# One attention + FFN kernel: attention output in natural token order, one store per FFN tile, and a last tile copied by two engines

## The chip, the cores and the metric

The kernel runs on one core of one Trainium2 chip. A core has five engines with instruction streams of their own: PE (TensorE, matmuls), DVE (VectorE), ACT (ScalarE), POOL (GpSimd) and SP (SyncE, which here only issues DMAs). They meet through semaphores. The metric is the device time of one execution in microseconds (us).

## The reference

Decayed linear attention over blocks of 64 tokens (4 batches, 8 heads, 768 tokens, head dimension 64), and on its output an FFN of 3072 tokens with a snake activation:

```python
for b in range(nb):                       # 12 blocks of 64 tokens
    qb, kb, vb = q[:, :, sl], k[:, :, sl], v[:, :, sl]
    intra = einsum('bhic,bhjc->bhij', qb, kb) * Dmask      # lam**(i-j) for i >= j
    intra = einsum('bhij,bhjd->bhid', intra, vb)
    inter = einsum('bhid,bhde->bhie', qb * lam_pow, kv_state)
    out[:, :, sl] = intra + inter
    kv_state = lam_block * kv_state + einsum('bhsd,bhse->bhde', kb * rev_pow, vb)

x = out.transpose(0, 2, 1, 3).reshape(3072, 512)
h = x @ w_in                              # 512 -> 2048
g = h + sin(alpha * h)**2 / (alpha + 1e-09)
y = g @ w_out                             # 2048 -> 512, fp32
```

## The kernel before

**Units and groups.** The attention is done in 24 units. A unit is 256 tokens of one batch and four heads, in two blocks of 128 tokens (index c). Four units (two batches, two halves of the heads) make a group g of 512 tokens; there are six groups. For each group the FFN has 16 FFN1 tiles (f, 128 of the 2048 channels by 512 tokens) and four FFN2 tiles (m, 128 tokens by 512 outputs).

**Tokens in pairs.** A load puts tokens 2p and 2p+1 of a block on the same partition ("(p two) e -> p h (two e)"), which makes 512-byte runs. So inside a block of 128 tokens the columns stand as two runs of 64, first the even tokens ("par" 0), then the odd ones. Before the change this order goes through the whole kernel: the scores, the attention output in PSUM (`okv`), the activations `xt`, the FFN. It is undone when the result is stored: `f2st` (L753) sends a tile in two DMAs, one per parity, of 64 partitions each.

**A unit's steps**, with the names in the written orders: `ldNq/k/v` loads (SP); `cqN`, `ckN` casts to bf16 and `svN` scaling of v (L490 to L498); transposes on PE with copies (`tqN`, `tkN`, `e0N`, `e1N`, L508 to L517) for the first nine units, a DMA transpose `dtN` for the others; `scN` scores (L532); `mmN` mask product (DVE, L540); k-v products (L566) with their copy `kcN` (`kv_copy`, L576, `kva`), `bxN`/`d0N`/`d1N`/`n0N`/`n1N` for the state (`kvbd`, L594, L608); `inN`, `ioN` the two output products (`intermm` L642 and `outmm` L655, both into `okv`); `oeN` the scaled read-out of `okv` by the table `ET` into `xt` (`outev`, DVE, L674). From unit 8 on, the PE part of a unit and the output part of the unit before are one `stepN`.

**FFN steps.** `f1_g_f` (L689, four matmuls), `sn` sine (ACT, L696), `sq` square (ACT L703 or POOL L705), `g_g_f` the product and sum into `gall` (DVE, L708); `f2_g_m_j` (L725, a quarter of the 16 matmuls of a tile), `ev_g_m` the copy of the tile out of PSUM to one of three output buffers `ob` (`f2ev`, L731, ACT), `out_g_m` its store (SP). The last tile (g 5, m 3) is done in two column halves `a` and `b`, with `end0`/`end1` as copies (`f2end`, L737, L739) and `send0`/`send1` as stores (`f2send`, L746). `warm` are filler matmuls (L762) of the start.

**The order.** Each engine's instructions stand in an order written out by hand (`SEQ`), a list of names for each engine. A small planner (`Plan.run`) walks these lists with a cost for each operation and a model of the DMA queues and of instruction fetches (`FETCH`); it only decides which buffer each operation takes and in which global sequence the operations are emitted. On an engine the written order is the order of execution, and so is SP's: a store that waits holds back every load and store behind it. SP's list ends so:

```
out_3_3 out_2_0 out_2_3 out_4_3 out_5_2 out_5_1 send1 send0 out_5_0
```

PE's ends with `f2_5_0_3 f2_5_3_2b f2_5_3_3b`, ACT's with `ev_5_2 end0 ev_5_1 ev_5_0`, DVE's with `g_5_9_None end1`.

Of the kernel before, what the change touches and what calls it, by code (L numbers as in the profile page):

```python
# [10 lines left out]
ALU = mybir.AluOpType  # L11
# [18 lines left out]
class Plan:  # L30
# [5 lines left out]
    FETCH = (4.0, 14.5, 21.5, 27, 48, 56, 66.5, 76.5, 86, 98.5, 108.5, 121, 131.5, 142.5, 157)  # L36
    HOLD, SHARE = 1.5, 0.35
# [108 lines left out]
def kernel(  # L146
# [28 lines left out]
            "warm warm warm warm lamb warm warm warm warm warm warm warm warm warm warm warm tq0 "  # L175
            "warm alpha tk0 warm warm warm tq1 warm tab0 kv0 sc0 tk1 warm tq2 warm warm warm sc1 "
            "warm tk2 kv1 in0 io0 sc2 warm kv2 warm in1 tq3 io1 warm tk3 in2 io2 sc3 kv3 warm warm "
            "tq4 in3 warm warm warm io3 f1_0_0_0 tk4 f1_0_0_1 f1_0_1_None sc4 kv4 f1_0_5_None in4 "
            "f1_0_2_None f1_0_3_None f1_0_4_None io4 f1_0_8_None f1_0_6_None f1_0_7_None f1_0_9_None "
            "f1_0_15_None f1_0_14_None f1_0_13_None f2_0_0_0 f2_0_1_0 f1_0_10_None f1_0_11_None "  # L180
            "f2_0_0_1 f2_0_3_0 f1_0_12_None f2_0_1_1 f2_0_1_2 f2_0_0_2 f2_0_0_3 tq5 f2_0_3_1 tk5 tq6 "
            "f2_0_1_3 sc5 tk6 f2_0_3_2 kv5 sc6 kv6 f2_0_3_3 tq7 in5 io5 tk7 f2_0_2_0 kv7 sc7 "
            "f2_0_2_1 in6 io6 f2_0_2_2 in7 io7 f2_0_2_3 f1_1_8_None f1_1_15_None tq8 f1_1_9_None "
            "f1_1_4_None f1_1_7_None f1_1_1_None f1_1_0_None tk8 f1_1_3_None step8 f1_1_2_None "
            "f1_1_5_None f1_1_10_None f1_1_6_None step9 f1_1_11_None f2_1_2_0 f2_1_0_0 f2_1_2_1 "
            "step10 f1_1_12_None f1_1_13_None f2_1_0_1 f2_1_0_2 step11 f1_1_14_None f2_1_1_0 "
            "f2_1_1_1 f2_1_1_2 step12 f2_1_0_3 f2_1_1_3 f1_2_15_None f1_2_3_None f1_2_4_None step13 "
            "f1_2_5_None f2_1_2_2 f1_2_6_None f2_1_2_3 f1_2_8_None f1_2_14_None f1_2_7_None f2_1_3_0 "
            "f2_1_3_1 step14 f1_2_0_None f1_2_13_None f2_1_3_2 f2_1_3_3 f1_2_12_None f1_2_2_None "
            "step15 f1_2_1_None f1_2_9_None f1_2_10_None step16 f1_2_11_None f2_2_1_0 f2_2_1_1 "  # L190
            "f1_3_15_None step17 f1_3_13_None f2_2_1_2 f1_3_12_None f2_2_1_3 f1_3_3_None f1_3_7_None "
            "f1_3_0_None f1_3_14_None step18 f1_3_11_None f2_2_2_0 f1_3_5_None f2_2_2_1 step19 "
            "f1_3_8_None f1_3_1_None f2_2_2_2 f1_3_10_None f2_2_2_3 step20 f1_3_6_None f1_3_4_None "
            "f1_3_2_None f1_3_9_None step21 f1_4_15_None f1_4_4_None f2_3_1_0 f2_3_1_1 step22 "
            "f1_4_6_None f1_4_11_None f2_3_1_2 f2_3_1_3 step23 f1_4_0_None f1_4_14_None f1_4_1_None "
            "f2_3_0_0 io23 f2_3_0_1 f2_3_0_2 f1_5_15_None f2_3_0_3 f1_5_14_None f1_5_3_None "
            "f1_4_10_None f2_3_2_0 f2_3_2_1 f1_4_5_None f1_4_7_None f2_3_2_2 f2_3_2_3 f1_4_3_None "
            "f1_5_4_None f1_4_12_None f1_4_2_None f2_3_3_0 f2_3_3_1 f1_4_8_None f1_5_6_None f2_3_3_2 "
            "f1_4_9_None f2_3_3_3 f1_4_13_None f2_4_2_0 f2_4_2_1 f1_5_1_None f1_5_8_None f2_4_2_2 "
            "f2_4_2_3 f1_5_12_None f2_4_0_0 f2_4_0_1 f1_5_0_None f2_4_0_2 f2_4_0_3 f2_4_3_0 "  # L200
            "f1_5_5_None f1_5_11_None f2_4_3_1 f1_5_2_None f2_4_3_2 f2_4_1_0 f2_4_1_1 f2_2_0_0 "
            "f2_4_3_3 f2_2_0_1 f1_5_7_None f2_4_1_2 f2_4_1_3 f1_5_13_None f2_2_3_0 f2_2_3_1 "
            "f1_5_10_None f2_2_3_2 f2_2_3_3 f2_2_0_2 f2_2_0_3 f1_5_9_None f2_5_1_0 f2_5_2_0 "
            "f2_5_3_0a f2_5_3_1a f2_5_2_1 f2_5_3_2a f2_5_3_3a f2_5_1_1 f2_5_2_2 f2_5_2_3 f2_5_1_2 "
            "f2_5_0_0 f2_5_1_3 f2_5_3_0b f2_5_3_1b f2_5_0_1 f2_5_0_2 f2_5_0_3 f2_5_3_2b f2_5_3_3b ",
        "DVE":
            "tabc tabm tab2 ck0 alphav tab4 mm0 e02 mm1 oe0 mm2 oe1 e13 oe2 bx3 mm3 oe3 e14 g_0_0_0 "
            "g_0_0_1 bx4 mm4 g_0_1_None g_0_5_None g_0_2_None g_0_3_None g_0_4_None g_0_8_None "
            "g_0_6_None g_0_7_None oe4 g_0_15_None g_0_14_None g_0_9_None g_0_10_None g_0_11_None "
            "g_0_13_None g_0_12_None e15 e06 mm5 bx5 bx6 mm6 oe5 bx7 mm7 oe6 oe7 e08 g_1_8_None "  # L210
            "g_1_15_None g_1_9_None g_1_4_None g_1_7_None e18 g_1_0_None g_1_1_None g_1_3_None mm8 "
            "g_1_5_None g_1_2_None g_1_6_None mm9 oe8 g_1_10_None g_1_11_None oe9 mm10 g_1_13_None "
            "g_1_12_None mm11 oe10 g_1_14_None oe11 mm12 g_2_15_None g_2_3_None g_2_4_None "
            "g_2_5_None mm13 g_2_6_None oe12 g_2_14_None g_2_7_None mm14 oe13 g_2_8_None g_2_0_None "
            "g_2_13_None g_2_12_None mm15 oe14 g_2_2_None g_2_1_None oe15 g_2_10_None mm16 "
            "g_2_11_None g_2_9_None g_3_15_None g_3_13_None mm17 g_3_12_None oe16 g_3_3_None "
            "g_3_7_None g_3_0_None oe17 mm18 g_3_14_None g_3_11_None g_3_5_None oe18 mm19 g_3_8_None "
            "g_3_1_None g_3_10_None oe19 mm20 g_3_4_None g_3_6_None g_3_2_None mm21 oe20 g_3_9_None "
            "g_4_15_None oe21 g_4_4_None mm22 g_4_6_None mm23 g_4_11_None oe22 g_4_1_None oe23 "
            "g_4_14_None g_4_0_None g_5_15_None g_5_14_None g_4_10_None g_5_3_None g_4_7_None "  # L220
            "g_4_5_None g_4_3_None g_5_4_None g_4_2_None g_4_12_None g_4_8_None g_5_6_None "
            "g_4_9_None g_4_13_None g_5_1_None g_5_8_None g_5_0_None g_5_12_None g_5_11_None "
            "g_5_2_None g_5_5_None g_5_7_None g_5_10_None g_5_13_None g_5_9_None end1 ",
        "ACT":
            "lam alq cq0 e00 cq1 e01 e10 kc0 tab3 e11 ck2 e12 kc1 cq3 kc2 ck3 e03 cq4 e04 kc3 "
            "sn_0_0_0 sq_0_0_0 sn_0_0_1 sq_0_0_1 sn_0_1_None kc4 sn_0_5_None sn_0_2_None sn_0_3_None "
            "sn_0_4_None sq_0_3_None sn_0_8_None sn_0_6_None sq_0_6_None sn_0_7_None sq_0_7_None "
            "sn_0_15_None sn_0_14_None sq_0_15_None sn_0_13_None sn_0_9_None sq_0_9_None "
            "sn_0_10_None sq_0_10_None sn_0_11_None sq_0_11_None sn_0_12_None sq_0_12_None cq5 cq6 "
            "e05 ev_0_0 ev_0_1 e16 kc6 kc5 e07 e17 ev_0_3 kc7 cq8 ev_0_2 sn_1_8_None sq_1_8_None "  # L230
            "sn_1_15_None sn_1_9_None sn_1_4_None sq_1_9_None sn_1_7_None sq_1_7_None sn_1_1_None "
            "sn_1_0_None sq_1_0_None sn_1_3_None sq_1_3_None kc8 sn_1_2_None sn_1_5_None sq_1_5_None "
            "sn_1_6_None sq_1_6_None sn_1_10_None kc9 sq_1_10_None sn_1_11_None sq_1_11_None ck12 "
            "kc10 sn_1_12_None sn_1_13_None sq_1_13_None sq_1_12_None kc11 cq13 sn_1_14_None ck13 "
            "sq_1_14_None kc12 cq15 cq14 ev_1_0 ev_1_1 sn_2_15_None sq_2_15_None sn_2_3_None "
            "sn_2_4_None kc13 sn_2_5_None sq_2_4_None sq_2_5_None sn_2_6_None sq_2_6_None ev_1_2 "
            "sn_2_8_None sn_2_14_None sn_2_7_None sq_2_14_None sq_2_7_None kc14 cq18 sn_2_0_None "
            "sn_2_13_None sq_2_0_None sq_2_13_None ev_1_3 sn_2_12_None sq_2_12_None sn_2_2_None kc15 "
            "sq_2_2_None sn_2_1_None sq_2_1_None sn_2_10_None kc16 sn_2_9_None sn_2_11_None "
            "sq_2_11_None ck18 sq_2_9_None sn_3_15_None kc17 sq_3_15_None sn_3_13_None sq_3_13_None "  # L240
            "sn_3_12_None cq20 ev_2_1 sn_3_3_None sn_3_7_None sn_3_0_None sq_3_7_None kc18 "
            "sn_3_14_None sn_3_11_None sq_3_11_None sn_3_5_None cq23 sq_3_5_None kc19 sn_3_8_None "
            "sq_3_8_None sn_3_1_None sn_3_10_None sq_3_1_None sq_3_10_None kc20 ev_2_2 sn_3_6_None "
            "sn_3_4_None sq_3_4_None sn_3_2_None sq_3_2_None sn_3_9_None sq_3_9_None kc21 "
            "sn_4_15_None sn_4_4_None sq_4_15_None kc22 sn_4_11_None sn_4_6_None sq_4_6_None kc23 "
            "ev_3_1 sq_4_11_None sn_4_0_None sn_4_1_None sq_4_1_None sn_4_14_None sq_4_14_None "
            "sn_5_15_None ev_3_0 sq_5_15_None sn_5_14_None sn_4_10_None sq_4_10_None sn_5_3_None "
# [192 lines left out]
    def tables_e(op):  # L440
        A.copy(out=ET[:], in_=tb0.tile[:])

# [629 lines left out]
```

## Time and profile before

| what | value |
|---|---|
| median of 3 runs | 218.9 us (218.4 to 218.98) |
| the profiled execution: its time, its span | 218.37 us, 216.6 us |
| granted TensorE clock, mean | 0.991 |
| busy: PE, DVE, ACT, POOL | 206.4, 119.4, 139.1, 131.4 us |
| filler matmuls (L762) in PE's busy time | 33 matmuls, 8.3 us |
| the chain that ended last, by engine | PE 87%, POOL 5%, DVE 2%, issue 2%, ACT 1% |
| stores | 46 of 128 KB, 4 of 64 KB |
| DMA | 33.65 MB, mean 155 GB/s |

The span goes from the first to the last instruction of the profiled execution; its own time is taken around that. Busy times come from instruction records. Matmul records overlap, as the next one starts before the last column of the one before has come out, so a group's start-to-start distance is its price on PE, not the duration of its records. A wait is put down to what ended it.

### The profile page before, as it was taken

How to read it: one execution, taken by the hardware profiler on the slowest of the kernel's cores; microseconds unless marked ns; L12 is line 12 of the kernel's file. 1: busy time of each engine (PE TensorE's matmuls, PEld its weight loads, DVE VectorE, ACT ScalarE, POOL GpSimd, SP SyncE). 2: the span in 40 equal slices, each digit the busy share in tenths (PEclk: the TensorE clock that was granted, in tenths of full speed). 3: DMA queues.
4: the chain of work that ended last, by engine and by line, in shares of the span. 5: the costliest groups of instructions: out<-in, count | busy, mean ns of one | idle time of the engine just before them, and what ended most of it. 6: DMA issues, size and time to landing. Idle time of an engine off the chain costs nothing.

```text
span 216.6 us, 5232 instructions
## 1 busy us (share of the span) xinstructions
PE 206.4 (95%) x2066; PEld 105.6 (49%) x2066; DVE 119.4 (55%) x174; ACT 139.1 (64%) x251; POOL 131.4 (61%) x212
## 2 busy tenths in 40 slices
PE   8889999999999999999999999999999999999970
PEld 3466444555445555455545555544444444445430
DVE  3487775385488754777958868773555223022000
ACT  3675788554998668979887787567587635442210
POOL 7999899488799789998979998231511120011000
PEclk9999999999999999999999999999999999999996
DMA  6999999999998999999888740042040120044424
GB/s 176 300 278 207 206 157 200 304 251 305 246 278 221 182 273 250 249 190 293 224 201 203 128 100 3 0 100 48 0 97 2 25 61 14 0 97 92 99 55 98
DMA packets 62139, 33.65 MB, mean 155 GB/s; under 512 B 17938, under 2 KB 59170, under 8 KB 62114
## 3 DMA queue, kind: packets, MB, share of 16 engines
q1 hardware_dynamic: 57776, 29.04, 57.9%
q0 software_dynamic: 4224, 4.19, 12.3%
q8 instruction: 16, 0.26, 0.5%
q10 hardware_dynamic: 114, 0.07, 0.1%
q14 instruction: 9, 0.07, 0.1%
HBM read 27.27 MB, written 6.29 MB: 155 GB/s over the span
## 4 chain that ended last, share of the span: by engine, by line
PE 87%; POOL 5%; DVE 2%; issue 2%; ACT 1%; POOLq 0%; DVEq 0%
PE hps L689 38%; PE ops L725 35%; PE okv L725 3%; PE sp L532 3%; PE okv L655 3%; PE okv L642 2%; POOL vb L498 1%; DVE gall L708 1%; PE okv L566 1%; PE pt L508 1%; POOL E L410 1%; ACT s L696 1%; ACT s L703 1%; DVE sm L540 1%; POOL w_in_sb L456 0%
## 5 line engine op out<-in xcount | busy, mean ns | idle before, releaser
L708 DVE SCALAR_TENSOR_TENSOR gall<-s,r_sb,hps 128x512 bf16<-128x512 bf16 (+1 forms) x97 | 69.6, 740 | 60.1 <-ACT s L703 42.9
L689 PE MATMUL hps<-xt,w_in_sb 128*128 128x512 bf16 (+1 forms) x388 | 91.7, 377 | 0.7 <-DVE gall L708 0.6
L696 ACT ACTIVATE s<-hps,alpha_sb 128x512 bf16<-128x512 f32 (+1 forms) x97 | 65.5, 680 | 29.0 <-PE hps L689 27.5
L725 PE MATMUL ops<-w_out_sb,gall 128*128 128x512 bf16 (+1 forms) x368 | 83.1, 370 | 0.0
L705 POOL TENSOR_TENSOR s<-s 128x512 bf16<-128x512 bf16 x31 | 32.1, 1041 | 49.3 <-ACT s L696 47.2
L725 PEld LDWEIGHTS <-gall 128*128 128x128 bf16 x400 | 38.5, 98 | 42.1 <-DVE gall L708 0.2
L689 PEld LDWEIGHTS <-w_in_sb 128*128 128x128 bf16 x388 | 36.4, 98 | 42.1 <-issue 1.8
L703 ACT ACTIVATE s<-s 128x512 bf16<-128x512 bf16 (+1 forms) x66 | 40.3, 621 | 1.2
L540 DVE TENSOR_TENSOR sm<-sp,mask 128x1024 bf16<-128x1024 f32 x24 | 29.2, 1218 | 1.0 <-PE sp L532 1.0
L498 POOL TENSOR_TENSOR vb<-st_v,R 128x512 bf16<-128x512 f32 x24 | 25.0, 1045 | 1.1 <-DMA st_v<-in_v_dram 0.9
L731 ACT COPY ob<-ops 128x512 f32<-128x512 f32 x21 | 12.2, 586 | 19.7 <-PE ops L725 19.7
L594 POOL TENSOR_TENSOR kvbd<-kvx,LBD 128x256 bf16<-128x256 f32 x32 | 19.7, 614 | 2.5
L674 DVE TENSOR_TENSOR xt<-okv,ET 128x512 bf16<-128x512 f32 x24 | 16.5, 687 | 6.1 <-ACT kva L576 3.6
L591 POOL TENSOR_TENSOR kvx<-kva,kvs 128x128 f32<-128x128 f32 x32 | 14.6, 456 | 7.3 <-ACT kva L576 7.2
L492 POOL CAST qk<-st_k 128x512 bf16<-128x512 f32 x18 | 10.9, 614 | 3.3 <-DMA st_k<-in_k_dram 3.2
L532 PE MATMUL sp<-qt 64*64 64x128 bf16 x384 | 10.1, 221 | 0.1
L655 PE MATMUL okv<-sm,vb 64*64 64x128 bf16 x384 | 9.7, 218 | 0.5 <-DVE sm L540 0.5
L490 ACT CAST qk<-st_q 128x512 bf16<-128x512 f32 x13 | 7.9, 619 | 3.1 <-DMA st_q<-in_q_dram 3.1
L576 ACT COPY kva<-okv 128x256 f32<-128x256 f32 (+1 forms) x16 | 5.1, 316 | 6.9 <-PE okv L566 6.9
L632 POOL TENSOR_TENSOR kvs<-kvx,ET 128x128 f32<-128x128 f32 x24 | 9.4, 404 | 0.0
L762 PE MATMUL bz<-const-bfloat16-1.0 128*128 128x256 bf16 (+1 forms) x33 | 8.3, 358 | 0.8 <-PEq L1056 0.8
L642 PEld LDWEIGHTS <-kvbd 128*128 128x128 bf16 x80 | 6.2, 98 | 5.3 <-POOL kvbd L594 0.5
(63 smaller groups left out, 109.5 us busy)
## 6 DMA issues: line engine op xcount, KB each, us to landing
st_k<-in_k_dram SPq DMA_DIRECT2D x24, 256.0 KB, 4.0
st_q<-in_q_dram SPq DMA_DIRECT2D x24, 256.0 KB, 5.1
st_v<-in_v_dram SPq DMA_DIRECT2D x24, 256.0 KB, 4.4
out_dram<-ob SPq DMA_DIRECT2D x46, 128.0 KB, 2.4
w_out_sb<-in_moe_w_out_dram POOLq DMA_DIRECT2D x4, 512.0 KB, 8.5
w_in_sb<-in_moe_w_in_dram POOLq DMA_DIRECT2D x2, 512.0 KB, 7.2
w_in_sb<-in_moe_w_in_dram POOLq DMA_DIRECT2D x1, 768.0 KB, 10.2
w_in_sb<-in_moe_w_in_dram POOLq DMA_DIRECT2D x1, 256.0 KB, 7.1
```

Source lines behind the costliest of these rows:

```text
L498: ENGINE[op.eng].tensor_tensor(out=T[u, "vb"][:], in0=T[u, "v"][:].rearrange("p h two e -> p two h e"), in1=R[:, :, hs].unsqueeze(3).to_br ...
L532: nc.tensor.matmul(out=T[u, "sp"][half[c], hd, par, hp, :], lhsT=QT[half[hd], 1, par, hp, half[c]], rhs=QT[half[hd], 0, :, hp, half[c]], s ...
L540: V.tensor_tensor(out=T[u, "sm"][:].rearrange("p hd par hp i -> p (hd par) hp i"), in0=T[u, "sp"][:].rearrange("p hd par hp i -> p (hd par ...
L594: G.tensor_tensor(out=bd[:], in0=X.unsqueeze(2).to_broadcast([P, 2, 2, D]), in1=LBD[:, hs, :].unsqueeze(3).to_broadcast([P, 2, 2, D]), op= ...
L655: nc.tensor.matmul(out=okv[half[hd], c, hp * P:(hp + 1) * P], lhsT=VB[half[c], par, 2 * hp + hd, :], rhs=ST[half[c], hd, par, hp, :], star ...
L674: V.tensor_tensor(out=o, in0=i, in1=ET[:, 2 * hh:2 * hh + 2].rearrange("p hp two e -> p hp (two e)") .unsqueeze(1).to_broadcast([P, 2, 2, ...
L689: op.ins = nc.tensor.matmul(out=op.tile[:, cols], lhsT=w_in_sb[:, c, f * P:(f + 1) * P], rhs=xt[g][:, c].rearrange("p b c i -> p (b c i)") ...
L696: A.activation(out=op.tile[:, cols], in_=mm.tile[:, cols], func=ACTF.Sin, scale=alpha_sb[:, f:f + 1])
L703: A.activation(out=op.tile[:, cols], in_=s1, func=ACTF.Square)
L705: ENGINE[op.eng].tensor_tensor(out=op.tile[:, cols], in0=s1, in1=s1, op=ALU.mult)
L708: V.scalar_tensor_tensor(out=gall[g][:, f, cols], in0=sq.tile[:, cols], scalar=r_sb[:, f:f + 1], in1=mm.tile[:, cols], op0=ALU.mult, op1=A ...
L725: op.ins = nc.tensor.matmul(out=first.tile[:, cols], lhsT=gall[g][:, f, m * P:(m + 1) * P], rhs=w_out_sb[:, f, cols], start=(f == 0), stop ...
```

## The change

- **Natural order.** The output products write `okv` with a step of two elements (`nat`), so that even and odd tokens interleave in PSUM. The table `ET` is stored in the same order, and the moving operand of `outmm` is written as two runs (the same addresses in the same sequence). `xt`, the FFN and the output tiles are then in token order.
- **One store per tile.** A store is one DMA of 128 partitions by 512 columns (256 KB).
- **The last quarter.** The last column half of the last tile is copied in two pieces of 128 columns, one by ACT (stored from ACT's queue), one by DVE (stored from SP's).
- **Engine choices.** `ev` and `kc` may be done by DVE as well.
- **Planner.** Store times and fetch times are other ones, and all five written orders are new. On DVE there are now eight `ev` (ev_0_2, ev_1_0, ev_1_2, ev_3_3, ev_4_0, ev_2_0, ev_5_2, ev_2_3) and six `kc` (11 to 14, 17, 22). PE has 32 `warm` in place of 33, 29 of them ahead of the first FFN1 tile.

The functions, without planner costs:

```diff
-    ET = consts.tile([P, HP, 2, D], FP32, name="ET")
+    ET = consts.tile([P, HP, P], FP32, name="ET")
...
-        A.copy(out=ET[:], in_=tb0.tile[:])
+        A.copy(out=ET[:].rearrange("p hp (e two) -> p hp two e", two=2), in_=tb0.tile[:])
...
+    def nat(a):
+        return a.rearrange("p (e two) -> p two e", two=2)
...
-                        out=okv[:, c, hp * P:(hp + 1) * P],
+                        out=nat(okv[:, c, hp * P:(hp + 1) * P]),
                         lhsT=sts[c][:, hp].rearrange("p two e -> p (two e)"),
...
-                            out=okv[half[hd], c, hp * P:(hp + 1) * P],
+                            out=nat(okv[half[hd], c, hp * P:(hp + 1) * P]),
                             lhsT=VB[half[c], par, 2 * hp + hd, :],
-                            rhs=ST[half[c], hd, par, hp, :],
+                            rhs=ST[half[c], hd, par, hp, :].rearrange(
+                                "p (two e) -> p two e", two=2),
...
-    def f2send(op, ev, g, m, cols, queues):
+    def rows_of(g, m):
         _, tp, b, _, _ = where(4 * g + 2 * (m // 2))
         r0 = b * S + tp * W + (m % 2) * C
-        rows = out[r0:r0 + C, cols].rearrange("(p two) d -> two p d", two=2)
-        for par in range(2):
-            queues[par].dma_start(out=rows[par], in_=ev.tile[par * D:(par + 1) * D, cols])
+        return slice(r0, r0 + C)
+
+    def f2send(op, ev, g, m, cols, queue):
+        queue.dma_start(out=out[rows_of(g, m), cols], in_=ev.tile[:, cols])
 
     def f2st(op, ev, g, m):
...
-        for par in range(2):
-            SY.dma_start(out=rows[par], in_=ev.tile[par * D:(par + 1) * D, :])
+        SY.dma_start(out=out[rows_of(g, m), :], in_=ev.tile[:])
...
-                ev = add("end1", on("DVE", .35), [prev], lambda op, first=first, cols=cols:
-                         f2end(op, first, cols), take=("ob",))
-                add("send1", on("SP", 1.0), [ev], lambda op, ev=ev, cols=cols:
-                    f2send(op, ev, g, m, cols, (SY, A)))
+                c0 = cols.start
+                for e, w, qu in (("ACT", slice(c0, c0 + 128), A), ("DVE", slice(c0 + 128, DM), SY)):
+                    ev = add("end" + e, on(e, .29), [prev], lambda op, first=first, w=w:
+                             f2end(op, first, w), take=("ob",))
+                    add("send" + e, on("SP" if e == "DVE" else e, .55), [ev],
+                        lambda op, ev=ev, w=w, qu=qu: f2send(op, ev, g, m, w, qu),
+                        dma=(.17, .08) if e == "DVE" else None)
```

The written orders, cut to their first and last lines (PE to its last):

```diff
 PE
-            "f2_5_3_0a f2_5_3_1a f2_5_2_1 f2_5_3_2a f2_5_3_3a f2_5_1_1 f2_5_2_2 f2_5_2_3 f2_5_1_2 "
-            "f2_5_0_0 f2_5_1_3 f2_5_3_0b f2_5_3_1b f2_5_0_1 f2_5_0_2 f2_5_0_3 f2_5_3_2b f2_5_3_3b ",
+            "f2_4_1_2 f2_5_1_0 f1_5_9_None f2_5_1_1 f2_4_1_3 f2_5_2_0 f2_2_3_0 f2_5_1_2 f2_5_1_3 "
+            "f2_5_2_1 f2_5_2_2 f2_5_2_3 f2_5_0_0 f2_2_3_1 f2_5_0_1 f2_5_0_2 f2_2_3_2 f2_2_3_3 "
+            "f2_5_0_3 f2_5_3_0a f2_5_3_1a f2_5_3_2a f2_5_3_3a f2_5_3_0b f2_5_3_1b f2_5_3_2b "
+            "f2_5_3_3b ",
 DVE
-            "tabc tabm tab2 ck0 alphav tab4 mm0 e02 mm1 oe0 mm2 oe1 e13 oe2 bx3 mm3 oe3 e14 g_0_0_0 "
...
-            "g_5_2_None g_5_5_None g_5_7_None g_5_10_None g_5_13_None g_5_9_None end1 ",
+            "tabc cq0 tabm ck0 tab2 e10 alphav mm0 tab4 mm1 e12 oe0 mm2 oe1 e03 oe2 mm3 bx3 e14 oe3 "
...
+            "g_5_2_None g_5_5_None g_5_10_None g_5_7_None ev_2_0 g_5_13_None g_5_9_None ev_5_2 "
+            "ev_2_3 endDVE ",
 ACT
-            "lam alq cq0 e00 cq1 e01 e10 kc0 tab3 e11 ck2 e12 kc1 cq3 kc2 ck3 e03 cq4 e04 kc3 "
...
-            "sn_5_10_None sq_5_10_None sn_5_13_None ev_2_3 ev_2_0 sn_5_9_None ev_5_2 end0 ev_5_1 "
-            "ev_5_0 ",
+            "lam cq1 e00 alq cq2 e02 ck1 e01 e11 kc0 ck2 tab3 kc1 cq3 kc2 ck3 e13 cq4 e04 kc3 "
...
+            "sq_5_2_None sq_5_5_None sn_5_10_None sn_5_7_None sn_5_13_None sn_5_9_None ev_4_1 ev_5_1 "
+            "ev_5_0 end0 endACT sendACT ",
 POOL
-            "iden tab1 tabi tabd sv0 ck1 cq2 bx0 sv1 wi0 sv2 bx1 wi1 bx2 sv3 wi2 wi3 ck4 n03 d13 sv4 "
+            "iden tab1 tabi tabd sv0 sv1 wi0 bx0 sv2 bx1 wi1 bx2 wi2 sv3 ck4 wi3 wo0 wo1 sv4 wo2 "
...
 SP
-            "ld0k ld0q ld1q ld0v ld1k ld2q ld1v ld2k ld2v ld3q ld3v ld3k ld4q ld4k ld4v ld5q ld5k "
...
-            "out_3_3 out_2_0 out_2_3 out_4_3 out_5_2 out_5_1 send1 send0 out_5_0 ",
+            "ld1q ld0q ld0k ld2q ld0v ld1k ld1v ld2k ld3q ld2v ld3k ld3v ld4q ld4k ld4v ld5q ld5k "
...
+            "dt20 dt21 ld23k out_2_1 out_2_2 dt22 dt23 out_3_0 out_3_2 out_3_1 out_4_2 out_3_3 "
+            "out_2_0 out_4_3 out_5_1 out_4_0 out_5_2 out_4_1 out_2_3 out_5_0 send0 sendDVE ",
```

## The prediction

> **What bounds the kernel now.** I read the page's busy shares first, then one table of three stretches cut where the PE (TensorE) becomes dense and where it ends.
>
> ```profile
> PE 206.4 (95%) x2066; PEld 105.6 (49%) x2066; DVE 119.4 (55%) x174; ACT 139.1 (64%) x251; POOL 131.4 (61%) x212
> ...
> 0.00:25.00 25.00, 21.96 (x338) 13.00 (x339) 14.96 (x34) 14.79 (x34) 22.13 (x43) 1.00 1.10 236
> 25.00:209.73 184.73, 184.39 (x1730) 92.58 (x1728) 104.02 (x140) 124.35 (x218) 109.25 (x170) 1.00 0.67 147
> 209.73:216.60 6.87, 0.01 (x1) 0.00 (x0) 0.42 (x1) 0.00 (x0) 0.00 (x0) 0.72 0.35 79
> ```
>
> The first number pair of a row is the stretch and its length, the next is PE busy. For 184.73 us PE idles 0.34 us, so nothing that other engines save there can come back as time. What is left are 25 us of start, where PE's busy time is partly filler matmuls, and 6.87 us after the last matmul. So I read the end in the timeline (start, duration):
>
> ```profile
> 203.37 0.38 ACT L737 COPY ob<-ops 128x256 f32<-128x256 f32 x1
> ...
> 208.94 0.59 ACT L731 COPY ob<-ops 128x512 f32<-128x512 f32 x1 [2.92 <-PE ops L725]
> 209.83 0.42 DVE L739 COPY ob<-ops 128x256 f32<-128x256 f32 x1 [11.26 <-PE ops L725]
> 210.28 1.75 SPq L746 DMA_DIRECT2D out_dram<-ob  x3
> 210.28 0.55 ACTq L746 DMA_DIRECT2D out_dram<-ob  x1
> 212.47 1.11 SPq L753 DMA_DIRECT2D out_dram<-ob  x2
> ```
>
> The column half copied at 203.37 and the tile copied at 208.94 have long been ready, but SP's written order has `send1` before `send0` and `out_5_0`. So five SP stores go out after the last copy, and the last begins only at about 213.0. The start is read in the chain of waits:
>
> ```profile
> 7.83 1.04 POOL vb L498
> 8.88 0.60 POOL qk L492 x2
> ...
> 10.56 1.00 POOL vb L498
> 11.56 0.90 POOL w_in_sb L456
> 12.49 1.07 POOL vb L498
> ...
> 17.51 1.14 DVE sm L540
> ```
>
> The POOL row at 8.88 is two casts. POOL scales v and issues the first FFN weights, and DVE's mask products follow. The first FFN matmul starts at 19.05 us.
>
> **The change part by part.** The profiled execution took 218.37 us around its 216.6 us span; the median is 218.9, so 0.53 is added at the end.
>
> *The end.* In the new orders SP stores `out_5_0`, then `send0`, then one last quarter (`sendDVE`); ACT stores the other. The last eight half-blocks of PE are both column halves of the last tile, 32 matmuls of 256 columns. Full 512-column matmuls go at 0.86 us for four (0.216 each, the chain's repeated row), so 256 columns take 0.108 and the 32 take 3.46 us. Counted back from PE's end, tile 5_0 is finished 3.46 us before, copied in 0.59 and issued in 0.6 (store issues: 0.47 to 0.6); `end0` starts 1.64 before and is sent by 0.65 before. SP is free when the last copies end. These are 128 columns each. ACT took 0.377 us for 256 and 0.587 for 512, so about 0.27; DVE 0.424 for 256 and 0.687 for the 512 of L674, so about 0.29. Do they run together? The table of waits has a row on that:
>
> ```profile
> DVE xt L674 <- ACT kva L576: 3.6, 4, 1.5
> ```
>
> `xt` does not use `kva`; both only read the same PSUM tile, in different columns. Two readers of a tile are put in sequence here, so I take the two copies one after the other: 0.09 (PE to copy, as at 209.83) + 0.29 + 0.06 + 0.27 + 0.03 = 0.74 us to the last issue (0.45 if together). From issue to landing the 64 KB stores took 2.0 and 2.2 us, and from the end of the last store's landing to the end of the span it is about 1.2 us: the last store is issued at 213.0, lands 2.3 to 2.4 later, and the span ends at 216.6. New tail: 0.74 + 2.0 + 1.2 = 3.9 us, between 3.4 (copies together, quick landing) and 4.5. Against 6.87 that is **-3.0 us** (-2.4 to -3.5). Three output buffers remain, and `endDVE` may take that of `out_5_0`. Issued about 2.9 before PE's end, this store has 3.0 us to land; 128 KB stores took 2.4 at the median, so a 256 KB one just fits. Were it 0.5 later, the tail would be 4.4, inside the bound.
>
> *One store per tile.* 46 issues of 588 ns become 23, so SP gains some 13 us:
>
> ```profile
> out_dram<-ob SPq DMA_DIRECT2D x46, 128.0 KB, 2.4
> out_dram<-ob SPq DMA_DIRECT2D x3, 64.0 KB, 2.0
> out_dram<-ob ACTq DMA_DIRECT2D x1, 64.0 KB, 2.2
> ```
>
> The packets keep their 2 KB rows, and the first loads, of 256 KB with four times as many rows, were issued in 0.47 to 0.51 us, so I count no dearer issue. The loads behind the stores can start earlier, but PE's 0.34 us of idle time says that no load is late: **0**, at most -0.3.
>
> *Work moved from ACT to DVE.* Eight evictions (about 0.69 each, by L674's 512 columns) and six copies of k-v products (0.42, by the 256-column copy) are 8.0 us more on DVE, which was busy 104.0 of 184.7 us in the dense stretch. Queued behind them are the `gall` products that free PE's banks; PE waited for `gall` twice, 0.6 us in all. DVE's idle time covers it; if a busy neighbourhood fails to, one such wait is 0.3 us. I take **+0.3**, up to +2 (seven waits), and not below -0.3, since no more idle time exists.
>
> *The start.* On POOL the casts of k1 and q2 (0.60 together in the chain's row at 8.88, plus 0.47 of waiting) go to ACT, and `sv1` comes directly after `sv0`, before `bx0`. So `sv1` starts at about 9.0 when its load has landed, and the first weights are issued at about 10.05 in place of 11.51. They took 7.1 us, so they land near 17.2, not 18.6. The attention side: q0's cast goes to DVE at 4.7, and the copy of k0's transpose to DVE too, so the first mask product starts near 7.7 and not 9.58. It then waits for others again: the second needs ACT's casts and copies (near 10.4, was 11.32), the third the first product's read-out (13.1, was 13.37), the fourth is at about 16.2 (was 17.43). Behind the fourth DVE now has `bx3` (0.41), on which unit 3's inter-block product waits. So its last output product moves from 18.70 to about 18.2, the first FFN matmul from 19.05 to 18.5. I take **-0.5** (-1.2 to +0.6; a load order that puts k0 third and k1 sixth can give it back). The four fillers fewer ahead of it lie beside these waits.
>
> *PSUM writes at a step of two.* 464 matmuls (80 at L642, 384 at L655) now write every other fp32 of `okv`. No row of this trace has a stepped matmul output. The nearest rows are these same matmuls with unit step:
>
> ```profile
> 103.13 0.39 PE L642 MATMUL okv<-qt,kvbd 128*128 128x128 bf16 x4
> 103.45 0.42 PE L532 MATMUL sp<-qt 64*64 64x128 bf16 x16
> 103.69 0.39 PE L655 MATMUL okv<-sm,vb 64*64 64x128 bf16 x16
> 103.92 0.29 PE L566 MATMUL okv<-vb,qk 64*64 64x64 bf16 x8
> ```
>
> From L655's start to the next group's it is 0.23 us for 16 matmuls, four at a time in the array's quadrants: 56 ns per round of 128 columns, what 0.216 us for 512 gives too (54). L532 reads its moving operand in two runs and goes at the same pace; that is a read, and says little of a write. The lower bound is **0**; nothing makes a stepped write faster. The upper bound is a doubled round. Units 5 to 23 lie in the dense stretch: 19 x 4 rounds x 56 ns = 4.3 us, and 16 x 4 + 3 x 2 = 70 matmuls of 55 ns = 3.9 us: +8.1 us. I take 0, by the nearest rows, and keep 8.1 as a rival. The Trainium skill (Advanced Engine Details and Errata, PSUM Cachelines) says that PSUM has lines of two fp32 values and that "Any non-contiguous AP significantly slows down matmuls". By that rule the sum would have the upper end; no row of this trace shows it or speaks against it.
>
> Sum: -3.0 + 0.3 - 0.5 = -3.2, so 218.9 - 3.2 = **215.7 us**; its own range, from the terms' bounds without the doubled round, is 214.2 to 217.6.
>
> **The rivals.** *Half-rate writes (slower).* If each stepped write takes two slots, PE gains 8.1 us of work exactly where it has no idle time: 215.7 + 8.1 = 223.8, a little less where a doubled round falls beside a wait, so about 223.5. For it: PE is the bound, so every ns counts. Against it: only that nothing here shows it. It decides from a round of 56 x (1 + 3.2/8.1) = 78 ns. *DVE becomes late.* The moved copies stand in front of `gall` products in groups 1 and 2, where DVE was busy 8.56 of the 10 us from 60 to 70. If each of the 14 cost PE 0.25 us, +3.5: about 218.9, on either side of the old time. Against it: four FFN banks let PE run ahead. *The end does not shrink as said.* The last stores wait for a buffer or land late, or PE's last blocks wait for gates: half of the end's gain, 217.2.
>
> **How the numbers follow.** Forecast 0.50; half-rate writes 0.28; DVE late 0.12 (faster 0.02, no change 0.06, slower 0.04); a half-shrunk end 0.10. A measurement of this kernel tells about 0.3% (0.7 us) from no change. Faster 0.50 + 0.10 + 0.02 = 0.62, same 0.06, slower 0.28 + 0.04 = 0.32. With nearly a third on the other side the range must take in the half-rate case: 214.0 to 224.0.
>
> **What would show it.** Right: nothing on SP between the last copy and the last store, the stretch after the last matmul near 3.9 us; L642 and L655 rounds still 55 ns apart; the first FFN matmul near 18.5; PE idle in the dense stretch under 0.7 us. Wrong: okv matmul groups that last 0.43 us in place of 0.23, several new waits of PE for `gall`, or a last store that waits for a buffer.

## The result, and the profile after

The changed kernel takes 225.2 us (median of 4 runs, 224.6 to 225.81) against 218.72 before: a ratio of 1.030, 95% interval 1.026 to 1.034. It is slower, where 215.7 was forecast; the time lies above the range, and 1.7 us above the 223.5 of the rival "half-rate writes". The profiled execution took 225.68 us, with a span of 223.9.

Busy shares on the page of the changed kernel, and its three stretches, cut again at 25 us and at the last matmul (stretch, length, then busy time of PE, PEld, DVE, ACT, POOL):

```profile
PE 215.6 (96%) x2065; PEld 111.4 (50%) x2065; DVE 127.6 (57%) x191; ACT 131.3 (59%) x233; POOL 135.6 (61%) x214
...
0.00:25.00 25.00, 21.13 (x328) 12.53 (x329) 14.61 (x34) 13.58 (x32) 19.96 (x39) 1.00 1.04 226
25.00:220.28 195.28, 194.51 (x1739) 98.88 (x1736) 112.72 (x157) 117.48 (x201) 115.69 (x176) 1.00 0.59 143
220.28:223.90 3.62, 0.00 (x1) 0.00 (x0) 0.29 (x1) 0.27 (x1) 0.00 (x0) 0.86 0.13 36
```

PE is still dense and still the bound, but it has 9.2 us more busy time with one matmul fewer. The end shrank as forecast, from 6.87 to 3.62 us; PE's last matmul came 10.55 us later. One unit's PE part in the dense stretch shows where the time went (timeline of the changed kernel: start, duration):

```profile
109.84 0.60 PE L649 MATMUL okv<-qt,kvbd 128*128 128x128 bf16 x4
110.37 0.42 PE L535 MATMUL sp<-qt 64*64 64x128 bf16 x16
110.61 0.61 PE L662 MATMUL okv<-sm,vb 64*64 64x128 bf16 x16
111.01 0.33 PE L569 MATMUL okv<-vb,qk 64*64 64x64 bf16 x8
```

From one group's start to the next group's start is what a group costs PE. The scores (L535), which write with unit step, still make room for the next group after 0.24 us. The two groups that write at a step of two don't: from L662 to L569 it is 0.40 us (0.23 before), and from L649 to L535 it is 0.53 us (0.32 before). Single L649 records start 109 ns apart, where it was 56. The end:

```profile
218.57 0.37 ACT L747 COPY ob<-ops 128x256 f32<-128x256 f32 x1 [1.16 <-PE ops L732]
218.97 2.00 SPq L757 DMA_DIRECT2D out_dram<-ob  x2
220.32 0.29 DVE L749 COPY ob<-ops 128x128 f32<-128x128 f32 x1 [3.67 <-PE ops L732]
220.69 0.27 ACT L747 COPY ob<-ops 128x128 f32<-128x128 f32 x1 [1.75 <-DVE ob L749]
220.98 0.38 ACTq L757 DMA_DIRECT2D out_dram<-ob  x1
```

SP has nothing queued when the last copies end. The two copies go one after the other: ACT's is released by DVE's (`<-DVE ob L749`). The start is later:

```profile
20.30 0.63 PE L662 MATMUL okv<-sm,vb 64*64 64x128 bf16 x16
20.87 0.61 PE L696 MATMUL hps<-xt,w_in_sb 128*128 128x256 bf16 x4
```

The first FFN matmul is at 20.87 us in place of 19.05. So PE's 10.55 us are 1.82 in the start and 8.7 after it; in the latter is one wait of 0.5 us that the kernel before does not have:

```profile
PE okv L732 <- DMA w_out_sb<-in_moe_w_out_dram: 0.5, 1, 0.5
```

### The profile page after: what moved, and what is told of

Its sections match the earlier page's. It is cut to its first block, busy times and chain, and to the rows that moved or that the text cites. A ratio compares the mean times of both kernels' runs of the same rounds, so it can differ in the third digit from the quotient of the medians.

```text
span 223.9 us, 5216 instructions
## 1 busy us (share of the span) xinstructions
PE 215.6 (96%) x2065; PEld 111.4 (50%) x2065; DVE 127.6 (57%) x191; ACT 131.3 (59%) x233; POOL 135.6 (61%) x214
## 4 chain that ended last, share of the span: by engine, by line
PE 78%; DMA 7%; POOL 5%; DVE 3%; issue 2%; ACT 2%; SPq 1%; POOLq 0%; ACTq 0%; DVEq 0%
PE ops L732 34%; PE hps L696 31%; PE okv L662 5%; DMA w_out_sb<-in_moe_w_out_dram 4%; PE okv L649 4%; POOL s L712 3%; DMA st_v<-in_v_dram 3%; PE sp L535 3%; SPq L475 1%; PE okv L569 1%; DVE sm L543 1%; ACT s L703 1%; DVE gall L715 1%; PE okv L732 1%; POOL kvs L636 1%
## 5 line engine op out<-in xcount | busy, mean ns | idle before, releaser
L712 POOL TENSOR_TENSOR s<-s 128x512 bf16<-128x512 bf16 x38 | 39.3, 1039 | 48.1 <-ACT s L703 47.8
L696 PEld LDWEIGHTS <-w_in_sb 128*128 128x128 bf16 x388 | 36.9, 98 | 43.3 <-issue 1.9
L710 ACT ACTIVATE s<-s 128x512 bf16<-128x512 bf16 (+1 forms) x59 | 35.9, 620 | 1.1
L739 ACT COPY ob<-ops 128x512 f32<-128x512 f32 x13 | 7.6, 587 | 18.9 <-PE ops L732 18.8
L662 PE MATMUL okv<-sm,vb 64*64 64x128 bf16 x384 | 14.8, 303 | 0.0
L649 PE MATMUL okv<-qt,kvbd 128*128 128x128 bf16 x80 | 12.7, 302 | 1.3 <-POOL kvbd L598 0.6
L518 ACT COPY qt<-pt 128x512 bf16<-128x512 bf16 x9 | 5.3, 584 | 12.7 <-PE pt L511 12.7
L741 DVE COPY ob<-ops 128x512 f32<-128x512 f32 x8 | 5.5, 689 | 11.0 <-DMA out_dram<-ob 5.5
L649 PEld LDWEIGHTS <-kvbd 128*128 128x128 bf16 x80 | 7.9, 114 | 6.2 <-POOL kvbd L598 0.8
L535 PE MATMUL sp<-qt 64*64 64x128 bf16 x384 | 10.0, 222 | 0.2 <-ACT qt L518 0.2
L662 PEld LDWEIGHTS <-vb 64*64 64x64 bf16 x384 | 9.1, 127 | 2.1 <-issue 2.1
## 6 DMA issues: line engine op xcount, KB each, us to landing
w_out_sb<-in_moe_w_out_dram POOLq DMA_DIRECT2D x4, 512.0 KB, 12.9
```

Of the source, the lines that this page charges most:

```text
L535: nc.tensor.matmul(out=T[u, "sp"][half[c], hd, par, hp, :], lhsT=QT[half[hd], 1, par, hp, half[c]], rhs=QT[half[hd], 0, :, hp, half[c]], s ...
L649: nc.tensor.matmul(out=nat(okv[:, c, hp * P:(hp + 1) * P]), lhsT=sts[c][:, hp].rearrange("p two e -> p (two e)"), rhs=T[u, "qt"][:, 0, :, ...
L662: nc.tensor.matmul(out=nat(okv[half[hd], c, hp * P:(hp + 1) * P]), lhsT=VB[half[c], par, 2 * hp + hd, :], rhs=ST[half[c], hd, par, hp, :]. ...
L696: op.ins = nc.tensor.matmul(out=op.tile[:, cols], lhsT=w_in_sb[:, c, f * P:(f + 1) * P], rhs=xt[g][:, c].rearrange("p b c i -> p (b c i)") ...
L710: A.activation(out=op.tile[:, cols], in_=s1, func=ACTF.Square)
L712: ENGINE[op.eng].tensor_tensor(out=op.tile[:, cols], in0=s1, in1=s1, op=ALU.mult)
```

## The experiments

The theory after this reading (A): a matmul write that steps takes two slots an element, and that is the loss (a slot is the time that PE has for one column, here 56/128 = 0.44 ns). The rival (B): the new orders and the work moved to DVE made PE late, and the longer rounds lie beside waits. "Before" in the ratios below is the kernel before, run on the same chip.

**The change without the step.** The output products write with unit step again, and so this kernel leaves out the natural order:

```diff
     def nat(a):
-        return a.rearrange("p (e two) -> p two e", two=2)
+        return a.rearrange("p (two e) -> p two e", two=2)
...
-        A.copy(out=ET[:].rearrange("p hp (e two) -> p hp two e", two=2), in_=tb0.tile[:])
+        A.copy(out=ET[:].rearrange("p hp (two e) -> p hp two e", two=2), in_=tb0.tile[:])
```

> The changed kernel with one thing taken back: the output products write okv with unit step again (and ET stands in that order); orders, stores and engines stay as changed. The un-pairing of the tokens is left out, so inside each 128 rows the even tokens come first. Theory A (a stepped write takes two slots): L649 and L662 rounds go from 109 back to 55 ns and PE's end comes 8.8 us earlier (464 records' worth: 80 x 54 ns + 96 rounds x 53 ns = 9.4, a little of it beside waits of the start): 225.2 - 8.8 = 216.4 us, 215.4 if the longer rounds also caused the later start. Rival B (the new orders and the work moved to DVE are what is late, the longer rounds lie beside waits): 222 us or more.

Measured: 216.77 us, ratio 0.989 (0.986 to 0.992). Rounds are at 56 ns, PE ends at 211.6 and not at 220.3, the first FFN matmul is at 19.64. Theory A holds, and B falls: with orders and moved work as changed, 8.4 us go with this one edit (8.9 if each kernel is taken against the kernel before that ran beside it).

```profile
104.97 0.39 PE L649 MATMUL okv<-qt,kvbd 128*128 128x128 bf16 x4
...
105.54 0.39 PE L662 MATMUL okv<-sm,vb 64*64 64x128 bf16 x16
105.76 0.29 PE L569 MATMUL okv<-vb,qk 64*64 64x64 bf16 x8
```

Here L662's 16 matmuls make room after 0.22 us again.

**The step alone, in the kernel before.** Only `nat` on both `okv` outputs, `ET` in that order, and a tile's two stores as rows 0 to 63 and 64 to 127:

```diff
-                        out=okv[:, c, hp * P:(hp + 1) * P],
+                        out=nat(okv[:, c, hp * P:(hp + 1) * P]),
...
-                            out=okv[half[hd], c, hp * P:(hp + 1) * P],
+                            out=nat(okv[half[hd], c, hp * P:(hp + 1) * P]),
```

> The kernel before with one part of the change alone: the output products write okv at a step of two, ET in natural order, the two stores of a tile take rows 0 to 63 and 64 to 127. Orders, number of stores and the end stay as before. Theory A: every round is 109 ns, +8.1 us for units 5 to 23 and up to 1 us more in the start: 218.7 + 8.1 = 226.8, up to 227.8 us. Rival B: no more than 220 us.

Measured: 227.38 us against 219.15, ratio 1.038 (1.035 to 1.041), that is +8.2. The same loss with the old orders, and in its trace the same distances: 0.53 us from the inter-block products to the scores, 0.40 from the other output products to the next group. What follows: the step's price doesn't hang on the orders.

**The end alone, in the kernel before.**

```diff
-            "out_3_3 out_2_0 out_2_3 out_4_3 out_5_2 out_5_1 send1 send0 out_5_0 ",
+            "out_3_3 out_2_0 out_2_3 out_4_3 out_5_2 out_5_1 send0 out_5_0 send1 ",
```

> The kernel before with only SP's last three names in another order: send0, out_5_0, send1. Theory (the end is a queue of stores on SP): after the last copy one store is left on SP and one on ACT; issue at 210.3, landing 2.1 later, 1.2 to the end: span 213.6, 3.0 us less, 215.7 us. Rival (the last landings take the time, not the queue): at most 1 us less, 217.7 us or more.

Measured: 216.61 us against 219.15, ratio 0.989 (0.986 to 0.993): -2.5 us, most of the end's gain from three names in a list. The stretch after the last matmul was 4.7 us and not 3.9: `out_5_0` is ready only 0.3 us before the last copy starts and still has two stores, so `send1` waits on SP until 212.41:

```profile
210.97 1.33 SPq L753 DMA_DIRECT2D out_dram<-ob  x2
211.25 0.42 DVE L739 COPY ob<-ops 128x256 f32<-128x256 f32 x1 [11.27 <-PE ops L725]
211.70 0.57 ACTq L746 DMA_DIRECT2D out_dram<-ob  x1
212.41 0.77 SPq L746 DMA_DIRECT2D out_dram<-ob  x1
```

**Writes in pairs.** What counts, contiguity or two neighbours at a time? The same number of elements, two neighbours and then a jump. The moving operands are still read in the sequence in which they lie; the tokens and their factors are mixed up inside each 128 rows, as this kernel leaves the natural order out:

```diff
-        return a.rearrange("p (e two) -> p two e", two=2)
+        return a.rearrange("p (e two t) -> p two e t", two=2, t=2)
```

> The changed kernel, but the output products write okv in pairs: two neighbouring fp32, then a jump of four. ET stays in natural order, so tokens and their factors are mixed up inside each 128 rows; counts and sizes of all instructions stay. Theory A1 (what counts is that two successive writes fall into the same 8 bytes): rounds of 55 ns, the time of the unit-step kernel, about 216.4 us. Rival A2 (any output that is not contiguous takes two slots an element): rounds of 109 ns, 225.2 us.

Measured: 217.11 us, ratio 0.991 (0.987 to 0.994), rounds at 56 ns: the unit-step time within the intervals. A1 holds in what it forecast: two neighbouring fp32 are enough, the jump between pairs costs nothing. A1's further claim, that the two have to fall into the same 8 bytes, was not tested: no run has a pair that doesn't.

**A step of four.** Again only the writes jump, and natural order is left out:

```diff
-        return a.rearrange("p (e two) -> p two e", two=2)
+        return a.rearrange("p (e two f) -> p two f e", two=2, f=2)
```

> The changed kernel with output products that write okv at a step of four fp32 in place of two (tokens stand in another order inside each 128 rows, ET not adapted). Theory A (a write that doesn't share its 8 bytes with the one before takes two slots, however far it jumps): rounds stay at 109 ns, 225 us. Rival (the price grows with the step, as banks would make it): rounds of 160 to 220 ns, 229 to 234 us.

Measured: 224.77 us (two runs), ratio 1.026 (1.021 to 1.030), rounds at 109 ns as with a step of two. The price doesn't grow with the step, at least not from two to four.

**The jump on the reading side.** Natural order can also be made where PE reads its moving operand from SBUF:

```diff
-                            out=T[u, "sp"][half[c], hd, par, hp, :],
+                            out=nat(T[u, "sp"][half[c], hd, par, hp, :]),
...
-                            rhs=QT[half[hd], 0, :, hp, half[c]],
+                            rhs=QT[half[hd], 0, :, hp, half[c]].rearrange("p two e -> p e two"),
```

(and the same for the inter-block products; `nat` here only names a contiguous output in pairs of tokens, and the mask is built in natural order).

> The changed kernel with natural token order made on PE's reading side: the scores' and inter-block products' moving operand is read in alternating jumps between the two runs of 64 (bf16 in SBUF, 512 bytes apart), okv and the scores are written with unit step, the mask is built in natural order. Theory (only the PSUM side pays): rounds of 55 ns at all three lines, 216.8 us, as with unit step. Rival (SBUF reads that jump at every element pay too): rounds of L532's counterpart and of the inter-block products near 109 ns, in the dense stretch 19 x 4 x 54 + 70 x 54 ns = 7.9 us more, 224.5 us.

Measured: 226.91 us, ratio 1.036 (1.032 to 1.040). The rival holds: reads that jump at every element pay too.

```profile
109.93 0.65 PE L649 MATMUL okv<-qt,kvbd 128*128 128x128 bf16 x4
110.50 0.68 PE L535 MATMUL sp<-qt 64*64 64x128 bf16 x16
111.02 0.39 PE L662 MATMUL okv<-sm,vb 64*64 64x128 bf16 x16
111.24 0.23 PE L569 MATMUL okv<-vb,qk 64*64 64x64 bf16 x4
```

The scores now hold PE for 0.52 us (0.24 before), while L662, whose reads and writes are both in order, is back at 0.22 (the last row is cut short where the window ends). Single L649 records start 122 ns apart, 66 more than with unit step. The rival had priced a round at 54 more; with 66 its 146 rounds are 9.6 us, and 216.8 + 9.6 = 226.4 is near what was measured.

**Natural order made by DVE**, on the way from PSUM to `xt`:

```diff
-            V.tensor_tensor(out=o, in0=i,
-                            in1=ET[:, 2 * hh:2 * hh + 2].unsqueeze(1).to_broadcast([P, 2, 2, P]), op=ALU.mult)
+            for c in range(2):
+                V.tensor_tensor(out=o[:, c].rearrange("p hp (e two) -> p hp two e", two=2),
+                                in0=i[:, c].rearrange("p hp (two e) -> p hp two e", two=2),
+                                in1=ET[:, 2 * hh:2 * hh + 2].rearrange("p hp (two e) -> p hp two e", two=2),
+                                op=ALU.mult)
```

> The changed kernel with unit-step products; natural order is made by DVE when it writes xt (bf16, step of two), in two instructions of 256 columns a unit in place of one of 512. Output in natural order, one store per tile. DVE gains 24 x (2 x 0.42 - 0.69) = 3.6 us, of which the chain of the start has 4 x 0.15 = 0.6 us on its path and the dense stretch nothing: 216.8 + 0.5 = 217.3 us, 1.5 us less than before. Rival (stepped bf16 writes cost DVE double): 24 x 0.5 more, read-outs late, 219 us or more.

Measured: 217.67 us, ratio 0.992 (0.989 to 0.995). The whole of what the change wants to do, faster than the kernel before by 1.3 us. The group's row:

```profile
L683 DVE TENSOR_TENSOR xt<-okv,ET 128x256 bf16<-128x256 f32 x48 | 18.6, 440 | 4.6 <-PE okv L662 2.9 <-PE hps L699 0.9 <-ACT kva L579 0.6
...
L612 DVE TENSOR_TENSOR kvbd<-kp,LBD 128x256 bf16<-128x256 f32 x3 | 1.3, 419 | 1.1 <-PE kp L569 1.1
```

It is 440 ns for 256 columns at a step of two. L612, the same kind of instruction with 256 fp32 columns from PSUM, writes its bf16 with unit step and took 419. So DVE's stepped bf16 writes are some 5% dearer at most.

**The end, in full, in the kernel before.** PE also finishes tile 5_0 ahead of the last column half:

```diff
-            "f2_5_0_0 f2_5_1_3 f2_5_3_0b f2_5_3_1b f2_5_0_1 f2_5_0_2 f2_5_0_3 f2_5_3_2b f2_5_3_3b ",
+            "f2_5_0_0 f2_5_1_3 f2_5_0_1 f2_5_0_2 f2_5_0_3 f2_5_3_0b f2_5_3_1b f2_5_3_2b f2_5_3_3b ",
...
-            "out_3_3 out_2_0 out_2_3 out_4_3 out_5_2 out_5_1 send1 send0 out_5_0 ",
+            "out_3_3 out_2_0 out_2_3 out_4_3 out_5_2 out_5_1 send0 out_5_0 send1 ",
```

> The kernel before with only the end in another order: PE does tile 5_0 before both column halves' last parts, SP sends send0, out_5_0, send1. All else as before, two stores per tile. Theory: at the last copy SP has nothing queued, the stretch after the last matmul goes from 6.9 to 3.8 us: 219.0 - 3.0 = 216.0 us, the lowest of all, as the start keeps its old order. Rival (PE waits elsewhere in the new end or the last tile's copy is late): 217.5 us.

Measured: 216.0 us against 218.97, ratio 0.986 (0.983 to 0.990). It beats both the kernel before and the changed kernel, with two stores per tile. Its stretches:

```profile
25.00:209.73 184.73, 184.39 (x1730) 92.49 (x1727) 104.02 (x140) 124.33 (x218) 108.91 (x170) 1.00 0.68 148
209.73:213.76 4.03, 0.00 (x0) 0.00 (x0) 0.42 (x1) 0.00 (x0) 0.00 (x0) 1.00 0.44 102
```

PE's end is that of the profile before to the hundredth; only what follows is shorter, 4.03 in place of 6.87 us.

**The start: v before q2 and k1.** This is the unit-step form with another order of the first loads; the natural order is left out:

```diff
-            "ld1q ld0q ld0k ld2q ld0v ld1k ld1v ld2k ld3q ld2v ld3k ld3v ld4q ld4k ld4v ld5q ld5k "
+            "ld1q ld0q ld0k ld0v ld1v ld2q ld1k ld2k ld3q ld2v ld3k ld3v ld4q ld4k ld4v ld5q ld5k "
```

> The unit-step form of the changed kernel (216.8 us, tokens not un-paired) with only the order of the first loads changed: v0 and v1 fourth and fifth, q2 and k1 sixth and seventh, in place of q2, v0, k1, v1. With unit step the new start orders gave no earlier first FFN matmul (19.64 and 19.12 us in two profiles, 19.05, 20.10 and 19.03 in three with the old orders), where -0.5 us was forecast; POOL waited 0.7 us twice for a v load. Theory (landing times set the start): POOL's first v product starts near 8.0, not 8.58, the second near 9.0, not 10.31, the first weights are issued near 10.0, not 11.29; but q2 and k1 land some 2 and 1 us later, and with them ACT's casts and the second mask product (11.6 to 12.5): first FFN matmul no earlier than 19.6, 216.8 to 218 us. Rival (POOL's order alone sets the start): first FFN matmul 1.2 us earlier, 215.6 us.

Measured: 218.74 us, ratio 0.999 (0.995 to 1.002), 2.0 us more than the unit-step form. POOL did start early, the first FFN matmul came late:

```profile
7.82 2.04 POOL L501 TENSOR_TENSOR vb<-st_v,R 128x512 bf16<-128x512 f32 x2
9.81 0.96 POOL L459 DMA_DIRECT2D w_in_sb<-in_moe_w_in_dram  x1
```

```profile
PE pt L511 <- ACT qk L493: 2.7, 1, 2.7
```

The first weights are issued 1.5 us earlier than in the unit-step form, and the first FFN matmul is at 21.63 and not 19.64. PE's wait of 2.7 us for q2's cast says why: the written order has q2's transpose ahead of the first scores. The rival falls: in these orders the landing of q2 holds the start, not POOL. What k1, moved with it, adds was not tested alone.

## Why the prediction was wrong

**The step that failed is the fifth term, "PSUM writes at a step of two": taken as 0, measured 8.2 to 8.9.** It is 8.2 us where the step alone is put into the kernel before, 8.4 to 8.9 where it alone is taken out of the changed kernel. Its upper end was right: rounds nearly doubled, and after the first FFN matmul PE had 8.7 us more, of which 152 rounds (units 4 to 23) at 109 - 56 = 53 ns are 8.1. What failed is the choice of 0 "by the nearest rows". These were the same matmuls with unit step, and so had no word on the matter; rows of what an edit takes away can't price what it puts in. The one statement that spoke of it, without a price, was the Trainium skill's (Advanced Engine Details and Errata, PSUM Cachelines). The measurement agrees with it for steps of two and four, and with its other sentence, "Every two consecutive elements should be contiguous for best throughput", by the pairs at 56 ns. It differs from its "Any non-contiguous AP", for the pairs are not contiguous as a whole. The rival's time of 223.5 was 1.7 us low: the price in the start was left out, and a gain of 0.5 in the start was counted in.

The range beside the sum does not come out either: the terms' own bounds, added up, give 213.6 to 219.1 and not 214.2 to 217.6. The result lies above both, so this decided nothing.

**The end** was right: -3.0 forecast, -3.25 measured (3.62 in place of 3.9). The two copies run in sequence, as the row `xt <- kva` let expect. Issues cost 0.33 to 0.38 us and landing 1.7, a little less than taken. The end alone, in the kernel before, gains 3.0 us.

**One store per tile: 0** fits what was measured, but no run tests it alone. 23 stores of 256 KB landed in 2.3 us at the median, no later than the 46 halves (2.4). No gain from the saved issue time shows: the fastest form, 216.0 us, has two stores a tile, and the unit-step form with one store, new orders and moved work together has 216.77.

**Work moved to DVE: +0.3** lies between what two profiles show. In the changed kernel PE never waited for it; in the unit-step form once, in the waits:

```profile
PE hps L696 <- DVE ob L741: 0.9, 1, 0.9
```

DVE as the late engine was not what happened.

**The start: -0.5** was wrong, +1.82 measured in the profiles. With unit step the first FFN matmul is at 19.64 and 19.12 us in two profiles, with the old orders at 19.05, 20.09 and 19.03: the new orders gain nothing that these profiles can tell. I had v1's product at 9.0; its load landed later, and it starts at 10.56 in the changed kernel. I had the first mask product at 7.7, and it starts at 9.30, for another reason: its scores had their operands copied at 7.02, but the new PE order has unit 2's q transposed ahead of them (`tq2` before `sc0`, the other way round before), and that waits for q2's cast:

```profile
PE pt L511 <- ACT qk L493: 1.5, 1, 1.5
```

What `tq2` behind `sc0` would give was not tested. Of the 1.23 us from the unit-step form to the changed one, 0.26 are there at the first output product already (13.22 and 12.96). The other 1.0 builds up over the stepped writes of units 0 to 3, whose output products stand one behind the other in this chain. I had left them out of the sum.

**Not foreseen:** the new order issues three of the four loads of the output weights from 19.45 to 22.7 us (before, all four were spread from 21.3 to 30.8), and their median landing went from 8.5 to 12.9 us. PE waited 0.5 us for `w_out`, and 1.6 us in the profile with pairs; in the unit-step form, with the same 12.9, it did not. That this order causes the late landing was not tested.

## What to carry to other kernels

A re-ordering is priced by the engine on whose access pattern it lands: on PE's output or moving operand it cost about a second slot per element (53 and 66 ns more on 56), on DVE's write some 5% at most. When an edit makes an access pattern that no row of the trace has, the rows it replaces are no evidence; take both ends seriously, or measure the one pattern first. And before any large change read the last few microseconds as a queue: here a few names moved in two written lists were worth 3.0 us.

## What the runs showed of the hardware

- PE writing fp32 to PSUM: 56 ns per 128 columns with unit step, 56 in pairs with a jump, 109 at a step of two and 109 at a step of four.
- PE reading bf16 from SBUF with a jump at every element: about 122 ns per 128 columns, 56 where the operand is two runs of 64.
- DVE writing bf16 at a step of two: 440 ns for 256 columns, 419 for the nearest unit-step row.
- A store of 128 partitions with 2 KB each is issued by SP in 0.38 us at the median (0.33 at the least, 23 stores of the changed kernel); one of 64 partitions in 0.59 (0.47 at the least, 46 stores of the kernel before), though it moves half as much.
- Two copies on different engines out of one PSUM tile were run in sequence, their starts 0.37 us apart. ACT waited there for the semaphore of DVE's copy, so it is the program that puts them in sequence; whether the chip could run them together was not tested.
